# Dividing the last unit's attention sums through 16 turned columns, with the output operations behind the second sum and new tables of order

## The chip, the cores and the metric

The kernel runs on one core of a Trainium2 chip. A core has five engines that work side by side, each through its own list of instructions in order: TensorE (PE in the profile, its weight loads PEld), VectorE (DVE), ScalarE (ACT), GpSimd (POOL) and SyncE (SP), which here only issues DMA transfers. They wait for one another by semaphores. Matmul results land in PSUM, operands lie in SBUF, and large intermediates go through device memory. The metric is the device time of one execution in microseconds (us), lower being better.

## The reference

A token stream x of 2048 x 448 goes through two branches that a gate mixes:

```python
g = sigmoid((x * gate_w).sum(-1, keepdims=True))
a = ssm_conv(x)          # long convolution, kernel K from 448 x 256 complex exponentials
b = infini_attention(x)  # 16 heads of 28, 4 segments of 512 tokens, memory across segments
return g * a + (1 - g) * b
```

In branch b, for each segment s and head: p = softmax(q k^T * scale + causal mask); a_dot = p v; a_mem = phi(q) M / (phi(q) z + 1e-6); o = sigmoid(beta) * a_mem + (1 - sigmoid(beta)) * a_dot; then M and z take up phi(k)^T v and the sum of phi(k). The outputs of the heads are multiplied by wo.

## The kernel before

**First half (to about 440 us).** `first_half` builds the convolution kernel K in 56 steps: per step PE computes arguments (`turns`, ps_arg), ACT takes sines and exponentials (cs, EY, EX), DVE multiplies them into X and Y, and PE sums (`sums`, ps_k). Between these steps `Feed.slot` inserts pieces of another stream, `project`: it splits wv, wq and wk into a high and a low part (`weights`: a load win on SP, a copy wsp on ACT, a difference wsp on POOL, a store to WD on SP, with two wsp buffers), computes q, k and v, stores them (QD, KD, VD), and builds the memory. The tables say how much is inserted at each of 190 slots: FEED (pieces of `project`), FILL (pieces of the Fourier transform of x, "fill" matmuls ut,s1u), VECTOR (1: this slot's copies run on DVE, otherwise on ACT), and UNREAD (short matmuls into ps_k ahead of each `sums`, whose result nobody reads). CHUNKS places the transform of K.

**Second half.** The order is written out by hand in the string PROGRAM, one letter per piece: l loads the q and k of a unit (4 heads of one segment; 16 units), A and B are its maxima, W its scores and exponentials (five steps and one of masking on POOL), V its product with v, E a piece of a segment's end (division by sums, output projection into TB, recall of the memory), C the convolution, b, j and z the inverse transform, D the division of one unit of the last segment (`divide`). t and T are fillers on PE: t is a matmul on a tile of ones into a ps_m tile (`turn_over`), T two half-array ones into a ps_a tile (`turn_halves`). There are two ps_m and three ps_a tiles.

**The end.** `last_end` (L1312) finishes the last segment: it projects the units 0 to 2 of four output tiles, runs the last V (pvs, copied out of PSUM by ACT, L1194), divides unit 3, projects it, and adds the result to yd, which holds the convolution's part. In `divide` (L1298) one matmul with `den`, 128 x 512, spreads each head's sum of exponentials over its 32 rows; DVE takes the reciprocal of 256 columns (L1308), scales pvs (L1309) and adds the memory's part am (L1310), and the same for the other 256 columns.

The stream of instructions of an engine is in the order in which the code issues it wherever the code asks for that (all of PE, the two followed engines of the first half); elsewhere a scheduler places it.

## Time and profile before

| | us |
|---|---|
| runs shown (3) | 811.17, 814.91, 815.10 |
| median of the runs | 814.91 |
| profiled execution, its own time | 806.25 |
| its span, first to last instruction | 804.3 |
| mean granted clock of TensorE | 0.976 of full speed |

The profile is one execution. Its rows name the line, the engine, the operation and the tiles (out<-in, buffer numbers left out). L1503 and L1506 are the helpers that issue every matmul and transpose, L1468 and L1489 those for copies and activations, L1519 and L1527 those for DMA, so the tile names tell the place. A bracket behind a row gives the idle time of its engine ahead of it and what ended that. The granted clock is the share of full speed at which TensorE ran. An fp32 matmul appears as two passes, each with its weight load.

### The profile page before, as it was taken

What the parts mean: (1) busy time and instruction counts of PE and PEld (TensorE: products, weight loads), DVE (VectorE), ACT (ScalarE), POOL (GpSimd) and SP (SyncE); (2) the same over time, 40 slices, a digit from 0 to 9 for tenths busy, and PEclk for the clock granted to TensorE, in tenths of its full rate; (3) what the DMA queues carried; (4) which work ended last, traced back from release to release, by engine and by line L of the source; (5) the groups of instructions that cost most, each with busy time, mean ns of one, the idle gap of its engine ahead of it and who ended that gap; (6) DMA issues with size and microseconds to landing.
All of it is one profiled execution on the core that took longest, in us unless ns stands there. A gap on an engine that the chain in (4) does not pass through costs nothing.

```text
span 804.3 us, 18905 instructions
## 1 busy us (share of the span) xinstructions
PE 714.8 (89%) x7374; PEld 393.9 (49%) x7374; DVE 564.0 (70%) x1123; ACT 552.9 (69%) x649; POOL 263.5 (33%) x314
## 2 busy tenths in 40 slices
PE   1676798999877998799999999999899999999897
PEld 1353455666444754466656344444444445444343
DVE  6979498867877867699679745555455656576585
ACT  3878689999997899999986166665466736642230
POOL 5404311111021011201121145575556646563120
PEclk9988999999998999999999999999999999999799
DMA  8626884367573357652777948596667787675784
GB/s 213 173 65 203 256 274 130 104 175 228 159 227 115 127 150 225 210 169 75 208 241 266 335 148 255 182 325 209 224 238 244 230 265 231 212 255 230 199 278 154
DMA packets 111970, 165.05 MB, mean 205 GB/s; under 512 B 27234, under 2 KB 76442, under 8 KB 111834
## 3 DMA queue, kind: packets, MB, share of 16 engines
q1 hardware_dynamic: 100058, 150.29, 59.2%
q10 hardware_dynamic: 7936, 9.64, 3.6%
q0 software_dynamic: 3888, 3.93, 1.8%
q8 instruction: 58, 0.95, 0.5%
q14 instruction: 30, 0.25, 0.1%
HBM read 99.67 MB, written 60.63 MB: 199 GB/s over the span
## 4 chain that ended last, share of the span: by engine, by line
PE 56%; ACT 16%; DVE 12%; issue 7%; DMA 6%; POOL 2%; SPq 1%; ACTq 0%; DVEq 0%; POOLq 0%
PE ps_m L1503 24%; PE ps_a L1503 22%; ACT cs L1468 6%; PE ps_k L1503 5%; PE ps_arg L1503 4%; DVE Y L402 2%; ACT L1468 2%; PE ps_m L1506 2%; DVE jk L1125 2%; DVE X L398 2%; ACT EX L1468 2%; DVE Y L403 1%; DVE Y L404 1%; DMA WD<-wsp 1%; DVE pin_f L223 1%
## 5 line engine op out<-in xcount | busy, mean ns | idle before, releaser
L1125 DVE CUSTOM_DVE_ANT_0 jk<-ps_a,mk 128x512 f32<-128x512 f32 (+3 forms) x256 | 125.4, 490 | 45.3 <-PE ps_a L1503 35.2
L368 POOL TENSOR_TENSOR EX<-EX,cab 128x1024 f32<-128x1024 f32 x28 | 53.5, 1913 | 227.4 <-ACT EX L1468 207.7
L1164 ACT ACTIVATE PT<-ps_a 128x1024 f32<-128x1024 f32 x80 | 81.0, 1023 | 53.7 <-PE ps_a L1503 52.5
L1468 ACT ACTIVATE cs<-ps_arg 128x1024 f32<-128x1024 f32 x111 | 107.5, 1023 | 2.4 <-DVE Y L403 2.0
L1503 PE MATMUL ps_m<-xh,w 128*128 128x512 f32 x224 | 81.1, 416 | 3.4 <-DMA w<-WD 3.3
L398 DVE TENSOR_TENSOR X<-EX,cs 128x1024 f32<-128x1024 f32 x56 | 68.3, 1220 | 18.5 <-ACT cs L1468 17.4
L1173 POOL TENSOR_SCALAR_AFFINE_SELECT PT<-PT 128x256 f32<-128x256 f32 (+1 forms) x96 | 46.5, 495 | 85.9 <-ACT PT L1164 74.9
L711 POOL TENSOR_TENSOR pr<-us,ks 128x896 f32<-128x896 f32 x32 | 67.6, 2112 | 20.8 <-ACT us L710 20.6
L1503 PE MATMUL ps_k<-Y,X 128*32 128x64 f32 x3584 | 63.9, 224 | 8.9 <-DVE Y L403 8.1
L402 DVE TENSOR_TENSOR Y<-EY,cs 128x1024 f32<-128x1024 f32 x56 | 70.1, 1251 | 0.0
L1503 PEld LDWEIGHTS ps_k<-Y,X 128*32 128x32 f32 x3584 | 54.4, 112 | 26.7 <-DVE Y L403 12.2
L1503 PE MATMUL ps_a<-qu,ku 64*128 64x256 f32 (+3 forms) x512 | 62.0, 353 | 0.6 <-DVE mx L1125 0.4
L1468 ACT ACTIVATE cs<-cs 128x1024 f32<-128x1024 f32 x56 | 59.3, 1059 | 1.8
L1503 PE MATMUL ps_m<-wz 128*128 128x512 bf16 x171 | 53.0, 390 | 5.5 <-ACT tb L1267 3.5
L404 DVE SCALAR_TENSOR_TENSOR Y<-EY,cs 128x512 f32<-128x512 f32 x56 | 42.8, 765 | 19.5 <-ACT cs L1468 16.9
L1468 ACT ACTIVATE EY<-ps_arg 128x1024 f32<-128x1024 f32 x52 | 52.1, 1041 | 3.9 <-PE ps_arg L1503 3.7
L1503 PEld LDWEIGHTS ps_m<-xh,w 128*128 128x128 f32 x224 | 42.0, 187 | 25.7 <-issue 10.8
L1503 PEld LDWEIGHTS ps_a<-qu,ku 64*128 64x128 f32 x512 | 41.8, 186 | 25.8 <-issue 13.3
L1503 PE MATMUL ps_m<-xl,w 128*128 128x512 f32 x128 | 50.2, 392 | 0.0
L1503 PEld LDWEIGHTS <-lh 64*128 64x128 bf16 x392 | 19.1, 95 | 55.2 <-issue 43.8
L1503 PE MATMUL ps_arg<-ce,lh 64*128 64x512 bf16 x168 | 35.9, 407 | 9.2 <-ACT EY L1468 3.3
L1503 PE MATMUL ps_arg<-ct,lh 64*128 64x512 bf16 x224 | 37.3, 389 | 7.2 <-ACT cs L1468 4.7
(219 smaller groups left out, 1419.3 us busy)
## 6 DMA issues: line engine op xcount, KB each, us to landing
ku<-KD SPq DMA_DIRECT2D x30, 512.0 KB
w<-WD SPq DMA_DIRECT2D x32, 448.0 KB
qu<-QD SPq DMA_DIRECT2D x15, 512.0 KB
GU<-gs SPq DMA_DIRECT2D x32, 224.0 KB
gk<-GK SPq DMA_DIRECT2D x32, 224.0 KB
gu<-GU SPq DMA_DIRECT2D x32, 224.0 KB
BB<-bs ACTq DMA_DIRECT2D x16, 448.0 KB
bt<-BB SPq DMA_DIRECT2D x8, 896.0 KB
```

The source lines that it names most:

```text
L223: x = op(*args, **kw)
L368: nc.gpsimd.tensor_tensor(o, o, cab, ALU.mult)
L398: v.tensor_tensor(X, ex, t[:, :, 0], ALU.mult)
L402: v.tensor_tensor(Y[:, :, :, :32], lo, y[:, :, :, ::-1], ALU.mult)
L404: v.scalar_tensor_tensor(Y[:, 1, :, 32:], ey[:, :, 32:], -1.0, y[:, 1], ALU.mult, ALU.mult)
L711: nc.gpsimd.tensor_tensor(pr[c], us, ks.pop(c), ALU.mult)
L1125: v.tensor_tensor_reduce(junk[:, :n], pt[:, x, o : o + n], k.mk[:, SEG - n :], 1.0, -3e38, ALU.add, ALU.max, mx[:, 3 - t, h : h + 1],)
L1164: nc.scalar.activation(to, x, AF.Exp, scale=SCALE)
L1173: nc.gpsimd.affine_select(sl, sl, pat, ALU.is_ge, 0.0, base=0, channel_multiplier=-1)
L1468: x = op(*args, **kw)
L1503: tc.keep_in_program_order(nc.tensor.matmul(*args, **kw))
L1506: tc.keep_in_program_order(nc.tensor.transpose(*args))
```

## The change

1. `last_end` calls the new `divide_last` in place of `divide(3)`. It computes the sums turned: pvs is the stationary operand and 4 columns of `den` the moving one, so 128 tokens lie on the rows and the 16 sums of four token blocks in 16 columns. DVE takes one reciprocal of 128 x 16 and copies it out to 128 x 512 (each value 32 times); four matmuls with the identity turn that back into the layout of pvs, and DVE scales straight from PSUM. Half of a projection is issued between the copy and the turning.
2. The four operations that add to yd are issued behind the last sum (`issue_after(x.ins)`).
3. FEED, FILL, UNREAD, VECTOR and PROGRAM have new values. FILL's sum goes from 33 to 48, UNREAD's from 218 to 242, VECTOR's from 82 to 81; FEED's stays at 249. PROGRAM has 129 t and 90 T instead of 171 and 56. CHUNKS is the same.

```diff
 FEED = (
-    2, 1, 1, 1, 0, 0, 4, 0, 1, 5, 5, 1, 0,
+    1, 2, 1, 0, 0, 4, 1, 0, 1, 5, 6, 0, 0,
...
+    def divide_last(meanwhile):
+
+        hg = 3
+        o = pvss[3][:, hg]
+        ds = k.ps("m")
+        for t in range(4):
+            at = k.den.rearrange("p (j e) -> p j e", e=32)[:, :, 0]
+            k.mm(ds[:, 4 * t : 4 * t + 4], o[:, 128 * t : 128 * t + 128], at, start=True, stop=True)
+        rc = ap.tile([128, 16], F32, tag="rcd", name="rcd", bufs=2)
+        v.reciprocal(rc, ds[:, :16])
+        rs = ap.tile([128, SEG], F32, tag="jk", name="rcb", bufs=1)
+        v.tensor_copy(rs.rearrange("p (j e) -> p j e", e=32), rc.unsqueeze(2).broadcast_to([128, 16, 32]))
+        meanwhile()
+        pb = k.ps("m")
+        for t in range(4):
+            c = slice(128 * t, 128 * t + 128)
+            k.mm(pb[:, c], rs[:, c], k.ident, start=True, stop=True)
+        x = None
+        for h in range(2):
+            c = slice(256 * h, 256 * h + 256)
+            with k.issue_after(x.ins) if x else ExitStack():
+                v.scalar_tensor_tensor(o[:, c], o[:, c], k.omg[:, hg : hg + 1], pb[:, c], ALU.mult, ALU.mult)
+            x = v.tensor_tensor(o[:, c], o[:, c], am[3][:, hg, c], ALU.add)
+        return x
...
         project(0, [2])
-        divide(3)
-        project(1, range(2))
+        x = divide_last(lambda: project(1, range(1)))
+        project(1, range(1, 3))
         for h in range(2):
-            project(h, [2, 3] if h else [3])
+            project(h, [3])
             for t in (2 * h, 2 * h + 1):
                 po, yd, i = pos[t], yds[t], 12 + t
-                v.scalar_tensor_tensor(yd, po, k.ogt[:, i : i + 1], yd, ALU.mult, ALU.add)
+                with k.issue_after(x.ins):
+                    v.scalar_tensor_tensor(yd, po, k.ogt[:, i : i + 1], yd, ALU.mult, ALU.add)
...
-bAWEbttWEVtWEEAEEAttttWtAEWETbbtEtttVTTTEEjjjjj
+TbAWAEbttWEVWEEAWtETTEttATTTTAEtWETbTEbTTTVTTEEjjjjj
```

The last pair of PROGRAM lines is the stretch near 740 us, the end of segment 2: the 39th E of PROGRAM, which projects the first tile of that segment, is the fifth E of the line in both.

The last instructions of DVE before: rcb is the reciprocal, pvs the last unit, yd an output tile.

```order
L1308 RECIPROCAL rcb<-ps_m 128x256 [waits PE_49]
L1309 SCALAR_TENSOR_TENSOR pvs<-pvs,omg,rcb 128x256 [waits DVE_49,Activation_49]
L1310 TENSOR_TENSOR pvs<-pvs,am 128x256 [waits DVE_49]
L1308 RECIPROCAL rcb<-ps_m 128x256
L1309 SCALAR_TENSOR_TENSOR pvs<-pvs,omg,rcb 128x256 [waits DVE_49]
L1337 SCALAR_TENSOR_TENSOR yd<-ps_a,ogt,yd 128x448 [waits DMAHW5_49,PE_49]
L1337 SCALAR_TENSOR_TENSOR yd<-ps_a,ogt,yd 128x448 [waits DMAHW6_49]
L1310 TENSOR_TENSOR pvs<-pvs,am 128x256 [waits DVE_49]
L1337 SCALAR_TENSOR_TENSOR yd<-ps_a,ogt,yd 128x448 [waits DMAHW7_49,PE_49]
L1337 SCALAR_TENSOR_TENSOR yd<-ps_a,ogt,yd 128x448 [waits DMAHW0_49]
```

The last instructions of DVE after, with rcd the reciprocal of 16 columns:

```order
L1321 RECIPROCAL rcd<-ps_m 128x16 [waits PE_49]
L1323 COPY rcb<-rcd 128x512 [waits DVE_49]
L1333 SCALAR_TENSOR_TENSOR pvs<-pvs,omg,ps_m 128x256 [waits PE_49,Activation_49]
L1334 TENSOR_TENSOR pvs<-pvs,am 128x256 [waits DVE_49]
L1333 SCALAR_TENSOR_TENSOR pvs<-pvs,omg,ps_m 128x256
L1334 TENSOR_TENSOR pvs<-pvs,am 128x256 [waits DVE_49]
L1363 SCALAR_TENSOR_TENSOR yd<-ps_a,ogt,yd 128x448 [waits DMAHW5_49,PE_49]
L1363 SCALAR_TENSOR_TENSOR yd<-ps_a,ogt,yd 128x448 [waits DMAHW6_49]
L1363 SCALAR_TENSOR_TENSOR yd<-ps_a,ogt,yd 128x448 [waits DMAHW7_49,PE_49]
L1363 SCALAR_TENSOR_TENSOR yd<-ps_a,ogt,yd 128x448 [waits DMAHW0_49]
```

The first two output operations moved from ahead of the second sum to behind it.

On PE, the end before and after (PT,V is the last V, wo,pvs a projection of one unit and tile):

```order
L1503 MATMUL ps_m<-PT,V 32x128 x4
L1503 MATMUL ps_a<-wo,pvs 128x448 x2
L1503 MATMUL ps_m<-pvs,den 128x512
L1503 MATMUL ps_a<-wo,pvs 128x448 x10
L1737 UNCONDITIONAL_BRANCH
```

```order
L1529 MATMUL ps_m<-PT,V 32x128 x4
L1529 MATMUL ps_a<-wo,pvs 128x448 x2
L1529 MATMUL ps_m<-den,pvs 128x4 x4
L1529 MATMUL ps_a<-wo,pvs 128x448 x2
L1529 MATMUL ps_m<-ident,rcb 128x128 x4
L1529 MATMUL ps_a<-wo,pvs 128x448 x8
L1763 UNCONDITIONAL_BRANCH
```

Ten projections follow the sums in both; two of them now stand between the sums and the turning, eight behind it.

On SP near 70 us, before and after (WD is the store of split weights, win the load of wk, lh a small operand of `turns`):

```order
L1527 DMA WD<-wsp_220 64x4x128
L337 DMA lh_85<-SP 24x2x128
L1527 DMA WD<-wsp_220 64x4x128
L337 DMA lh_85<-SP 24x2x128 x3
L1527 DMA win<-in_B_wk 128x448 x3
L1527 DMA win<-in_B_wk 64x448 x2
L853 DMA w<-WD 128x896 x2
```

```order
L1553 DMA WD<-wsp_220 64x4x128
L1553 DMA win<-in_B_wk 128x448
L1553 DMA WD<-wsp_220 64x4x128
L1553 DMA win<-in_B_wk 128x448
L337 DMA lh_85<-SP 24x2x128 x4
L1553 DMA win<-in_B_wk 128x448
L1553 DMA win<-in_B_wk 64x448 x2
```

Two loads of wk moved ahead of the four lh loads.

On ACT at the same place, from the gs copy on, before and after:

```order
L1468 ACTIVATE gs<-ps_m 128x448
L1468 ACTIVATE cs<-ps_arg 128x2x2x256 x2
L1468 ACTIVATE cs<-cs 128x1024
L1468 ACTIVATE wsp_219<-win 128x4x4x28
L1468 ACTIVATE wsp_220<-win 128x4x4x28
L1468 ACT_TABLE_LOAD
L1468 ACTIVATE EY<-ps_arg 128x1024
```

```order
L1494 ACTIVATE gs<-ps_m 128x448
L1494 ACTIVATE wsp_219<-win 128x4x4x28
L1494 ACTIVATE wsp_220<-win 128x4x4x28
L1494 ACTIVATE cs<-ps_arg 128x2x2x256 x2
L1494 ACTIVATE cs<-cs 128x1024
L1494 ACT_TABLE_LOAD
L1494 ACTIVATE EY<-ps_arg 128x1024
```

The two wsp copies moved ahead of three cs activations.

## Prediction

> **What bounds the kernel now.** I read the page first, then a table of stretches, then the chain of waits at three places: the start, the pocket near 745 us, and the end.

> The head of the page, its share of the chain, and its row of granted TensorE clock in 40 slices (tenths of full speed):

> ```profile
> span 804.3 us, 18905 instructions
> PE 714.8 (89%) x7374; PEld 393.9 (49%) x7374; DVE 564.0 (70%) x1123; ACT 552.9 (69%) x649; POOL 263.5 (33%) x314
> ...
> PEclk9988999999998999999999999999999999999799
> ...
> PE 56%; ACT 16%; DVE 12%; issue 7%; DMA 6%; POOL 2%; SPq 1%; ACTq 0%; DVEq 0%; POOLq 0%
> ```

> TensorE (PE) is busy 89% of the span and carries 56% of the chain, so time is PE time, unless PE waits. The next table gives, for each stretch, its length and the busy time of PE, its weight loads, DVE, ACT and POOL, then the granted clock and the share of the DMA engines:

> ```profile
> 80.00:102.30 22.30, 16.66 (x129) 10.45 (x129) 10.96 (x14) 14.78 (x17) 7.27 (x5) 0.92 0.81 259
> 440.00:745.00 305.00, 296.79 (x1962) 140.50 (x1963) 179.55 (x594) 164.06 (x191) 165.13 (x213) 1.00 0.72 240
> 747.00:757.00 10.00, 10.00 (x53) 3.27 (x52) 3.19 (x5) 1.51 (x2) 2.45 (x5) 0.56 0.70 181
> 757.00:804.30 47.30, 41.70 (x241) 17.84 (x233) 33.18 (x44) 10.90 (x12) 5.82 (x11) 0.99 0.73 220
> ```

> The second half (from 440 us) has PE busy 296.8 of 305.0 us, but part of that is filler: the letters t and T of PROGRAM issue matmuls on a tile of ones whose result nobody reads. So a busy PE there is either at real work or covering a wait of another engine. Outside it three places matter: the start, where PE is idle 5.6 of 22.3 us; 747 to 757, where PE is busy throughout at a clock of 0.56; and the last 47 us, with 5.6 us of idle PE.

> **The change part by part.** The profiled execution took 806.25 us (span 804.3). The runs shown have a median of 814.91 us, 8.7 us above it, so I sum differences on the profiled execution and subtract them from the median.

> *Start: the wk split.* The chain there, in order of time (start, us, what):

> ```profile
> 72.43 5.20 DMA win<-in_B_wk
> ...
> 77.67 3.57 POOL wsp L837 x2
> ...
> 81.26 6.63 DMA WD<-wsp
> ...
> 87.99 0.58 ACT wsp L1468
> ```

> Four links follow one another: load of a block of wk, split on POOL, store to WD, and a copy of the next block which needs the freed buffer. The same in the timeline, with the wait that it puts on ACT in brackets, and the group row of an ACT copy to hi:

> ```profile
> 68.56 0.66 SPq L1527 DMA_DIRECT2D WD<-wsp  x1
> ...
> 73.42 0.54 ACT L1468 ACTIVATE gs<-ps_m 128x448 f32<-128x448 f32 x1 [2.63 <-PE ps_m L1503]
> ...
> 86.01 0.58 ACT L1468 ACTIVATE wsp<-win 128x448 fp32r<-128x448 f32 x1 [5.39 <-DMA WD<-wsp]
> ...
> 92.14 1.02 ACT L1468 ACTIVATE EX<-ps_arg 128x1024 f32<-128x1024 f32 x1 [0.83 <-PE ps_arg L1503]
> ```

> ```profile
> L1468 ACT ACTIVATE hi<-ps_m 128x512 fp32r<-128x512 f32 x13 | 7.8, 598 | 0.7 <-PE ps_m L1503 0.7
> ```

> ACT stands 5.39 us behind the store. In the changed FEED two of the wk loads leave SP directly behind the two small WD stores at 68.56 us, ahead of four small loads of lh; the load that the chain shows at 72.43 can then start at about 70.0, and the first two wsp copies stand behind gs (73.42) instead of behind three more cs activations. The chain gains about 72.43 - 70.0 = 2.4 us, and I add 0.1 for the first load, which lands earlier still: 2.5 us. Against it, ACT now waits for the load in front of cs work, and VECTOR moves two hi copies from DVE to ACT, 2 x 0.60 = 1.2 us, right behind the EX that follows the copy. One of the two fits into the 0.83 us that ACT waited at 92.14. Net -2.5 + 0.6 = **-1.9 us**. Bounds: -5.4, if the whole wait goes, and +1.2, if the earlier load only moves ACT's wait and both copies are paid. The lh loads that are passed are small and belong to later steps; I give them no price. Later moves in the first half (a fill matmul, a projection, a copy traded between ACT and DVE, 24 more short ps_k fillers in UNREAD) exchange equal work within a step or two; I put them at nothing, covered by ACT and PE which alternate as the bound; without cover a copy costs its 0.6 us.

> *Fillers of the second half.* A run of six t, a run of five T (two half-array matmuls each) and what follows:

> ```profile
> 455.19 1.47 PE L1503 MATMUL ps_m<-wz 128*128 128x512 bf16 x6
> 456.59 1.25 PE L1503 MATMUL ps_a<-wz 64*128 64x512 bf16 x10
> 457.50 0.59 PE L1503 MATMUL ps_a<-ku,qu 64*128 64x256 f32 x4
> ```

> From start to start a t costs (456.59 - 455.19) / 6 = 0.23 us and a T (457.50 - 456.59) / 5 = 0.18, so I take 0.23 for either. PROGRAM has 171 t and 56 T before, 129 and 90 after: 8 fewer. By place it is 5 more inside the pocket near 740 (below), 2 fewer at its end, and so 11 fewer elsewhere: at most 11 x 0.23 = 2.5 us. Where a filler covered a wait its loss buys nothing. No row says which; I take half, **-1.3 us**, between 0 and -2.5.

> *The pocket near 745.* Idle time and its cause stand in brackets; r<-RD is the DMA that POOL issues when the reciprocals of segment 3 have come back from memory:

> ```profile
> 733.73 0.79 PE L1503 MATMUL ps_a<-qu,ku 64*128 64x384 f32 x8
> 734.45 0.39 PE L1503 MATMUL ps_m<-wz 128*128 128x512 bf16 x1
> ...
> 738.00 0.53 POOL L1208 DMA_DIRECT2D r<-RD  x1 [4.91 <-DMA RD<-rs]
> ...
> 745.95 0.63 ACT L1267 ACTIVATE tb<-ps_m,ogt 128x448 f32<-128x448 f32 x1 [5.74 <-DMA TB<-tb]
> 746.63 0.59 PE L1503 MATMUL ps_m<-wz 128*128 128x512 bf16 x1 [3.53 <-ACT tb L1267]
> 747.15 0.79 PE L1503 MATMUL ps_m<-r,sel 8*128 8x512 f32 x1
> 747.87 1.46 PE L1503 MATMUL ps_m<-wz 128*128 128x512 bf16 x3
> ```

> POOL stands 4.91 us behind RD, so xt of the next tile is late, its store is late, ACT's tb waits 5.74 us for that store, and PE 3.53 us for tb. That chain starts at the output projection of tile 0 (39th E) and is untouched. The changed words put one step of scores (W, 734.45 - 733.73 = 0.72 us) ahead of it: the chain ends 0.72 us later. The t that stood at 746.63 is gone, 747.15 - 746.63 = 0.52 us, and one of six fillers behind it, 1.46 / 3 = 0.49 at this clock. Net 0.72 - 0.52 - 0.49 = **-0.3 us**. PE reaches the wait later by the 5 further fillers, 5 x 0.23 = 1.15 us, so it idles 3.53 + 0.72 - 1.15 = 3.1 us, which is still long.

> How long a wait lowers the clock shows at another place, an idle stretch and the one behind it:

> ```profile
> 338.80:341.40 2.60, 0.03 (x1) 0.00 (x0) 0.63 (x2) 2.53 (x4) 0.58 (x1) 1.00 0.63 224
> 342.50:345.00 2.50, 2.35 (x12) 1.99 (x12) 2.50 (x4) 2.47 (x4) 0.00 (x0) 0.56 0.50 170
> ```

> After 2.6 us of idle PE the granted clock was 0.56, so I leave the 0.56 of 747 to 757 as it is. [...]

> *The end.* The chain, then three durations for the new operations: a reciprocal of 16 columns, a one-pass SBUF operation of 512 columns, and eight passes of 128 columns with what follows them on PE:

> ```profile
> 789.90 0.87 PE ps_m L1503 x2
> ...
> 790.80 1.77 DVE rcb L1308
> ...
> 793.61 1.68 DVE rcb L1308
> ...
> 796.98 0.34 DVE pvs L1310
> ...
> 797.37 2.54 PE ps_a L1503 x6
> ```

> ```profile
> 790.60 5.58 PE L1503 MATMUL ps_a<-wo,pvs 128*128 128x448 f32 x14
> ```

> ```profile
> L1050 DVE RECIPROCAL gt<-gt 128x16 f32<-128x16 f32 x1 | 0.3, 253 | 0.0
> ```

> ```profile
> L896 DVE TENSOR_SCALAR e<-e 128x512 f32<-128x512 f32 x24 | 10.3, 464 | 4.6 <-ACT e L1468 4.6
> ```

> ```profile
> 150.13 1.16 PE L1503 MATMUL ps_m<-v,pkT 128*128 128x128 f32 x8 [0.32 <-ACT pkT L1468]
> 151.04 0.46 PE L1503 MATMUL ps_m<-wvh,xh 128*128 128x450 f32 x1
> ```

> Before: sums of exp ready at 790.77, two reciprocals of 1.77 and 1.68 us on DVE, and PE idle until the second half is added (797.32); six passes then end at 799.91. After: four matmuls of 4 columns (8 passes) replace the one of 512. Eight passes of 128 columns take 151.04 - 150.13 = 0.91 us, and PE can hardly go slower with 4 columns, so the sums stand at about 790.8 as before. The reciprocal is 0.25 us, the copy 0.46 (to 0.7): rs is there at 791.7. PE meanwhile does four passes of projection; 14 passes in 5.58 us are 0.40 at most, so it is free at 792.3. The turning takes another 0.91, to 793.2, and two scale and add pairs of 0.95 us end at 794.2 and 795.1. PE still has 16 passes, 6.4 us, hence to 799.6, and never meets the later sums: the bound at the end passes from DVE to PE. 799.91 - 799.6 = 0.3; since 0.40 a pass is an upper bound (0.37 would make it 0.9), I take **-0.5 us**. The output operations now stand behind the second sum, where two of them stood ahead of it. The price is that the first two stores leave about 2 us later, close to the last two: up to +0.5 if the four share the way out. Bounds of this part: -1.2 and +0.8 (PE at twice 0.91 for the new matmuls).

> Sum: -1.9 - 1.3 - 0.3 - 0.5 = **-4.0 us**, that is 806.25 to 802.2, and 814.9 to **810.9 us**.

> **The rivals.** *A: only the end counts.* The tables exchange work that some other wait hides, at the start because SP's loads, with the DMA engines at 0.81 of their time (80 to 102 us), arrive no earlier. Then -0.5: 814.4 us. For it: the amounts of work on every engine are the same. Against it: the 5.39 us on ACT have one named cause, and that is moved.

> *B: the pocket gets short enough for the clock.* If 3.1 us of idling keeps the clock, the 10 us at 0.56 give back 10 x 0.44 = 4.4 us: 810.9 - 4.4 = 806.5 us. [...] Against it stands the row with 2.6 us.

> *C: slower, by the ps_a buffers.* T takes one of three ps_a tiles, which scores and maxima also take, where t takes ps_m. The runs of T go from 33 to 43 and those of t from 94 to 79. If every new run of T waits for one reader of its buffer (an exp on ACT takes 1.02 us by the EX row's size), that is 10 x 1.02 = 10.2, and -4.0 + 10.2 = +6.2: 821.1 us. It decides from 4.0 / 10 = 0.4 us a run on. Against it: PE's row of the second half shows 8 us idle in 305, with 33 such runs in it.

> **How the numbers follow.** 0.5% of 814.9 is 4.1 us, about what a measurement of this kernel can tell from no change. My forecast has 0.45: its own range is -7.5 to -1.5 (start between -4.4 and -0.5, fillers between 0 and -2.5), 807.4 to 813.4, and the sum lies at the edge, so it splits into 0.23 faster and 0.22 same. A has 0.18 (same), B 0.15 (faster), C 0.17 (slower); 0.05 is for what I name in none of them, 0.03 of it faster and 0.02 slower. Together faster 0.41, same 0.40, slower 0.19. The range reaches past B by some of the forecast's own width and halfway to C: 803 to 818.

> **What would show each step.** Start: ACT's wait of wsp for WD under 3.5 us and the first PE work behind the third w load about 2 us ahead of 102.3. Fillers: PE idle from 440 to 745 us grows by less than 1.3 us while the stretch gets shorter. Pocket: PE's wait for tb near 3 us and a clock near 0.56 behind it (B: near 1.00). End: no PE idle between the sums and the last projection, and the output operations directly behind PE. The prediction is wrong if T's own waits in ps_a add up to over 4 us (C), if ACT's wait at the start only moves to the wk load, or if a new idle of PE of over 2.6 us appears with a half clock behind it.

## The result and the profile after

| | before | changed |
|---|---|---|
| median of 17 runs each, side by side | 814.55 us | 805.70 us |
| lowest and highest | 808.66, 817.97 | 800.71, 810.18 |
| the profiled execution, its own time (span) | 806.25 (804.3) | 810.18 (808.5) |

The ratio is 0.990 (95% interval 0.9876 to 0.9923): 8.9 us faster by the medians, 8.1 us by the ratio. A second set, 12 runs of the changed kernel against 23 of the one before, gave 0.9927 (0.9898 to 0.9955). So the gain lies at 6 to 9 us (the two intervals reach from 3.7 to 10.1), and the prediction (-4.0 us, range 803 to 818) had the sign and was about half the size. Of all executions shown here one, of the kernel with the covered pocket below, took 1321.34 us and is left out of its ratio and its median.

The two profiled executions say the opposite: the changed kernel's span is 4.2 us longer. They are one execution each, and from opposite ends: 806.25 lies below all 17 runs of before, and 810.18 is the slowest of the 17 of the changed kernel. Subtracting these spans would have led astray, so in what follows a stage is compared over all the executions that a profile was taken of (14 in the end).

The head of the page of the changed kernel, and its four stretches (length, busy us of PE, weight loads, DVE, ACT and POOL, granted clock, DMA share and GB/s):

```profile
span 808.5 us, 19012 instructions
...
PEclk9987999999999999999999999999899999999889
...
PE 50%; ACT 20%; DVE 12%; DMA 7%; issue 6%; SPq 2%; POOL 2%; ACTq 0%; DVEq 0%; POOLq 0%
```

```profile
80.00:102.30 22.30, 18.18 (x137) 10.63 (x136) 10.32 (x14) 16.96 (x20) 6.09 (x4) 0.95 0.88 281
440.00:745.00 305.00, 291.94 (x1959) 141.79 (x1974) 179.15 (x588) 163.26 (x190) 164.85 (x212) 0.99 0.71 236
745.00:757.00 12.00, 11.19 (x61) 3.96 (x59) 4.18 (x7) 3.29 (x5) 2.44 (x5) 0.59 0.71 181
757.00:808.50 51.50, 43.68 (x240) 19.73 (x240) 30.36 (x44) 9.75 (x11) 5.82 (x11) 0.93 0.67 200
```

The start has 1.5 us more PE work in the same 22.3 us. The clock behind the pocket is about as low as before (0.59). New is the last row: a clock of 0.93 in the last 51 us, where before had 0.99.

**Where the time went, stage by stage.** The marks are starts of rows: the 5th, 13th, 21st and 29th multiplication X on DVE (L398), the first maximum jk (L1125, the second half begins), the 97th, 161st and the last jk, the first matmul of the last V, and the end of the span. The means are taken over profiled executions of all kernels below: in the first five rows over those whose first half is wholly old or wholly new, in the next four over those with the old or the new PROGRAM (without the three that edit the pocket or a load of bt), in the last over those with the old or the new end:

| stage | old | new | difference, us |
|---|---|---|---|
| start to 5th X | 98.07 (3) | 96.22 (7) | -1.9 |
| 5th to 13th X | 53.12 | 56.76 | +3.6 |
| 13th to 21st X | 53.98 | 54.62 | +0.6 |
| 21st to 29th X | 58.13 | 53.42 | -4.7 |
| 29th X to first jk | 178.98 | 177.54 | -1.4 |
| first to 97th jk | 90.10 (6) | 87.99 (5) | -2.1 |
| 97th to 161st jk | 88.89 | 89.98 | +1.1 |
| 161st to last jk | 127.41 | 127.53 | +0.1 |
| last jk to last V | 41.82 | 43.03 | +1.2 |
| last V to the end | 18.48 (7) | 17.82 (7) | -0.7 |

In brackets is the number of executions; it holds for the rows below it up to the next bracket. The first half gains 3.8 us, most of it between the 21st and the 29th X, in a place to which the prediction gave nothing. The words (PROGRAM) gain 2.1 us at the beginning of the second half, and the later rows have it back. The end gains what it was predicted to.

### The profile page after: what moved, and what is told of

It is laid out like the page before. It is cut to its first block, busy times and chain, and to the rows that moved or that the text cites. A ratio compares the mean times of both kernels' runs of the same rounds, so it can differ in the third digit from the quotient of the medians.

```text
span 808.5 us, 19012 instructions
## 1 busy us (share of the span) xinstructions
PE 713.1 (88%) x7415; PEld 398.9 (49%) x7438; DVE 561.3 (69%) x1122; ACT 552.5 (68%) x650; POOL 263.5 (33%) x314
## 4 chain that ended last, share of the span: by engine, by line
PE 50%; ACT 20%; DVE 12%; DMA 7%; issue 6%; SPq 2%; POOL 2%; ACTq 0%; DVEq 0%; POOLq 0%
PE ps_m L1529 21%; PE ps_a L1529 21%; ACT cs L1494 7%; PE ps_k L1529 4%; DVE jk L1125 4%; PE ps_arg L1529 3%; ACT L1494 2%; DVE X L398 2%; PE ps_m L1532 2%; DVE Y L402 2%; ACT EX L1494 2%; SPq L337 1%; ACT EY L1494 1%; DMA bt<-BB 1%; DVE Y L403 1%
## 5 line engine op out<-in xcount | busy, mean ns | idle before, releaser
L1125 DVE CUSTOM_DVE_ANT_0 jk<-ps_a,mk 128x512 f32<-128x512 f32 (+3 forms) x256 | 125.4, 490 | 50.8 <-PE ps_a L1529 41.1
L398 DVE TENSOR_TENSOR X<-EX,cs 128x1024 f32<-128x1024 f32 x56 | 69.3, 1237 | 18.4 <-ACT cs L1494 17.5
L404 DVE SCALAR_TENSOR_TENSOR Y<-EY,cs 128x512 f32<-128x512 f32 x56 | 40.7, 727 | 18.3 <-ACT cs L1494 15.9
L1529 PE MATMUL ps_a<-ku,qu 64*128 64x512 f32 (+3 forms) x256 | 41.7, 383 | 1.8 <-DVE mx L1125 1.3
L1140 POOL DMA_DIRECT2D qu<-mn x64 | 32.6, 516 | 29.4 <-ACT mn L1135 27.0
```

Of the source, the lines that this page charges most:

```text
L398: v.tensor_tensor(X, ex, t[:, :, 0], ALU.mult)
L404: v.scalar_tensor_tensor(Y[:, 1, :, 32:], ey[:, :, 32:], -1.0, y[:, 1], ALU.mult, ALU.mult)
L1125: v.tensor_tensor_reduce(junk[:, :n], pt[:, x, o : o + n], k.mk[:, SEG - n :], 1.0, -3e38, ALU.add, ALU.max, mx[:, 3 - t, h : h + 1],)
L1140: k.pdma(q[r : r + 1].bitcast(F32), mn[2 * j : 2 * j + 2, b].bitcast(F32))
L1529: tc.keep_in_program_order(nc.tensor.matmul(*args, **kw))
```

## The experiments

Each was timed beside the kernel before on the same chip. Ratios are to before. They are taken from all the runs of a set and are not the quotient of the medians; the medians of before were 812.71 us in the set of the first table below, 812.77 in that of the second table and of the covered pocket, and 813.49 in the last. The kernels have 12 runs each, where nothing else is said.

**Which part carries it.** Four kernels take the change apart: the new division and output order with all old tables; all new tables with the old division; the first half's tables alone (FEED, FILL, UNREAD, VECTOR); PROGRAM alone. The edit of the first as a diff against the kernel before is the diff of the functions shown above without the tables; of the second:

```diff
-        x = divide_last(lambda: project(1, range(1)))
-        project(1, range(1, 3))
+        divide(3)
+        project(1, range(2))
         for h in range(2):
-            project(h, [3])
+            project(h, [2, 3] if h else [3])
```

> Only the last unit's division and the place of the output operations are changed; all five tables are those of before. The two profiles at hand give, from the start of the last V's product on PE to the end of the span, 804.3 - 785.9 = 18.4 us before and 808.5 - 790.7 = 17.8 us after. Theory 1 (the terms of the prediction were each too small): about -0.6 us, no difference that can be measured, 811 to 816 us at a median of before of 814.5. Theory 2 (the end carries the gain): -4 us or more. Theory 3 (the gain is the tables'): 0, like theory 1.

> All five new tables, with the old division of the last unit. Theories 1 and 3: -8 us against before, so the new tables alone make it faster, about 806.5 us. Theory 2 (the end carries half or more): -4 us or less, 810 us or later.

> Only FEED, FILL, UNREAD and VECTOR are new: the first half; the words and the end are those of before. The prediction's start term is -1.9 us and it gives the other moves of the first half nothing, so by it 812.6 us. Theory 3a (the first half carries the gain, because the start's whole wait of 5.39 us goes and the later moves gain too): -5 us or more, 809.5 us or less. Theory 3b (the words carry it): -2 us or less.

> Only PROGRAM is new: the order of the second half. The prediction's terms for it are -1.3 us (fillers) and -0.3 us (pocket), so 812.9 us. Theory 3a: as that, -1.6 us or less. Theory 3b (the words carry the gain, by fewer waits or by a clock that keeps longer): -5 us or more, 809.5 us or less. If the parts are independent, end_alone, first_alone and words_alone add up to about -8.9 us.

| kernel | median | ratio to before |
|---|---|---|
| the end alone | 812.77 | 0.9982 (0.9955 to 1.0009) |
| the end undone | 806.76 | 0.9935 (0.9909 to 0.9962) |
| the first half's tables alone | 808.34 | 0.9953 (0.9924 to 0.9983) |
| PROGRAM alone | 813.01 | 0.9994 (0.9972 to 1.0016) |

The end does not carry the gain (theory 2 falls). The first half does (0.0047 x 813 = 3.8 us, theory 3a, though less than the 5 us it named), and PROGRAM by itself is worth nothing that can be measured: 0.5 us, in an interval from 2.3 faster to 1.3 slower, which also holds the 1.6 us of the prediction. Its profile does have the last V 2.7 us closer to the first jk (343.2 against 345.9 us); the lower half of the stage table shows what becomes of that.

**Which part of the first half.** FEED's running sums of before and after meet at many slots, so the tables can be exchanged in pieces. Three kernels on the base of before: slots 0 to 21 with the first ten numbers of UNREAD (the start); slots 73 to 85 (the middle, which acts between the 21st and the 29th X); slots 86 to 189 with UNREAD from the 15th number on (the rest of the first half). The new numbers of slots 22 to 72, among them one more transform of x at slot 31, and the 14th of UNREAD are in none of the three. The middle, in full, over slots 73 to 85 of each table:

```diff
-FEED    0, 1, 3, 2, 1, 1, 1, 1, 1, 0, 1, 1, 0
+FEED    0, 1, 0, 1, 3, 3, 0, 2, 1, 0, 1, 1, 0
-FILL    0, 0, 0, 0, 0, 1, 0, 0, 0, 0, 0, 0, 0
+FILL    1, 0, 0, 0, 0, 1, 0, 0, 0, 0, 0, 0, 1
-VECTOR  0, 1, 1, 1, 0, 0, 0, 1, 1, 1, 1, 0, 0
+VECTOR  1, 0, 1, 1, 0, 0, 0, 1, 1, 1, 1, 0, 0
```

> Before, with the new numbers of the first 22 slots of FEED and VECTOR and the first 10 of UNREAD, up to where FEED's sums meet again (21 pieces): the wk loads and copies of the start. In three profiles of the old first half the step of X that holds the start's wait (from the 4th to the 5th X on DVE) took 20.7, 21.9 and 19.4 us, in three of the new one 18.1, 17.4 and 17.9. Theory S (the prediction's start term, a little larger): that step takes about 18 us, and the time falls by 2 to 3 us, about 810.5 us. Theory M (the later moves of the first half carry it): the step gets shorter, but the next steps give it back, and the time falls by less than 1.5 us.

> Before, with the new numbers of FEED, FILL and VECTOR in slots 73 to 85 only: one transform of x more at slot 73 and one at 85, and eight pieces of the projection some slots later. Before, PE idled 3.25 us at 245 us behind DVE, with a half clock behind it, and the steps of X from the 26th to the 29th took 25.4 us (26.3 and 26.6 in two more profiles); in the changed kernel 22.2. Theory M: these three steps fall to about 22 to 23 us, the half clock there goes, and the time falls by 3 to 4 us, about 809.5 us. Theory S: no more than 1 us.

> Before, with the new numbers of FEED, FILL and VECTOR from slot 86 on and of UNREAD from the 15th on. In the profiles the steps from the 29th X to the first maxima of the second half took 179.4, 179.2 and 178.4 us with the old tables and 177.1, 177.5 and 177.5 with the new ones. Both theories: -1.5 to -2 us, which the profile shows and five rounds hardly do (812.5 us); -4 us or more would mean that the late moves carry the gain.

| kernel | median | ratio to before |
|---|---|---|
| the start alone | 809.26 | 0.9980 (0.9950 to 1.0009) |
| the middle alone | 809.03 | 0.9955 (0.9929 to 0.9982) |
| slots 86 on alone (6 runs) | 824.06 | 1.0130 (1.0102 to 1.0159) |

The middle, two transforms of x, seven pieces of the projection moved by one or two slots (by a count of FEED) and two numbers of VECTOR, gives 0.0045 x 812.8 = 3.7 us by itself, as theory M said. What it does is seen on PE. First before, then the kernel with the middle alone (start, us, engine, line, operation, tiles; idle time and its cause in brackets):

```profile
243.71 1.10 PE L1503 MATMUL ps_k<-Y,X 128*32 128x64 f32 x64
244.75 0.39 PE L1503 MATMUL ps_arg<-ce,lh 64*128 64x512 bf16 x2
248.39 1.11 PE L1503 MATMUL ps_m<-ut,s1u 64*128 64x448 f32 x1 [3.25 <-DVE lo L882]
248.40 1.03 PE L1503 MATMUL ps_arg<-ce,lh 64*128 64x512 bf16 x2
```

```profile
246.88 1.10 PE L1503 MATMUL ps_k<-Y,X 128*32 128x64 f32 x64
247.91 0.60 PE L1503 MATMUL ps_arg<-ce,lh 64*128 64x512 bf16 x3
248.14 0.91 PE L1503 MATMUL ps_m<-ut,s1u 64*128 64x448 f32 x2
248.89 0.92 PE L1503 MATMUL ps_arg<-ce,lh 64*128 64x512 bf16 x3
```

Before, the transform (ut,s1u) needs a ps_m tile which DVE frees only with lo, and all of PE stands in order behind it. DVE's copy of the transform ahead of it, gs, which frees another such tile, comes later still; in the kernel with the middle alone it comes 2.9 us earlier, so that its tile is free in time (before, then the middle alone):

```profile
248.25 0.61 DVE L1468 COPY gs<-ps_m 128x448 f32<-128x448 f32 x1
```

```profile
245.31 0.61 DVE L1468 COPY gs<-ps_m 128x448 f32<-128x448 f32 x1
```

ACT's next operation is the copy of the waiting transform's result, so ACT stands too (before):

```profile
250.28 0.54 ACT L1468 ACTIVATE gs<-ps_m 128x448 f32<-128x448 f32 x1 [4.08 <-PE ps_m L1503]
```

With the middle changed the transform finds its tile free, and neither waits. The stall was followed by 6.8 us at a granted clock of 0.50 (247.2 to 254.0 us), and that is gone as well, as a stretch that ends ahead of the same v,pkT shows in both (before, then the middle alone; the stretch does not begin with the same work):

```profile
235.00:261.00 26.00, 19.86 (x325) 11.54 (x313) 21.10 (x32) 20.65 (x25) 3.82 (x2) 0.87 0.34 111
```

```profile
235.00:259.50 24.50, 19.86 (x351) 12.24 (x351) 23.80 (x35) 23.82 (x29) 3.83 (x2) 1.00 0.52 160
```

From the transform ahead of the stall to that v,pkT it is 261.5 - 239.3 = 22.2 us before and 259.9 - 242.4 = 17.5 with the middle alone. The other profiles agree: between the 21st and the 29th X all five kernels with the old middle have a wait of PE for lo of 2.7 to 3.5 us (3.0 us and at an earlier transform where the start alone is new), and in none of the nine with the new middle does PE wait more than 1.8 us there. Which of the three tables' numbers does it was not separated.

The rest of the first half alone was the surprise: 11 us slower, where either theory had 2 us faster. Its profile loses 8 us between the 37th and the 45th X against the changed kernel and 5.4 against before (58.8, 50.8 and 53.4 us), where six passes, three transforms of x, stand from 351.27 on that the changed kernel has done before this place; DVE, with their copies, frees ps_m tiles late, and PE waits:

```profile
351.27 1.40 PE L1503 MATMUL ps_m<-ut,s1u 64*128 64x448 f32 x3
...
367.46 0.66 PE L1506 MATMUL ps_m<-ident,xin 128*128 128x128 f32 x4 [1.36 <-DVE lo L882]
370.84 1.11 PE L1506 MATMUL ps_m<-ident,xin 128*128 128x128 f32 x4 [2.73 <-DVE lo L884]
```

In the changed kernel the first of these waits is not there and the second is 0.24 us. Two of these three transforms are the middle's, and the third is that of slot 31. With all three moved ahead the changed kernel has issued all 32 transforms by 336 us (40th X), so that the new numbers of FILL from slot 144 on (43rd X) find nothing left; in the kernel with slots 86 on alone they draw the last three together. So the new numbers from slot 86 on seem to rest on the earlier ones; the pieces do not add up, and pieces of such a table cannot be priced one by one. That the missing three transforms are the whole reason was not tried, and 3.5 us of the loss lie elsewhere, between the 21st and the 29th X (61.6 us, where the mean of the old is 58.1).

**The start, in the whole.** The changed kernel with the old numbers in slots 0 to 21, beside a repeat of the changed kernel:

> The changed kernel with the old numbers in the first 22 slots of FEED and VECTOR and the first 10 of UNREAD: it undoes the start alone. Theory S (the start's earlier wk loads are worth 2 to 3 us in the whole): 2 to 3 us slower than the changed kernel, about 808 us, and the step from the 4th to the 5th X back at 19.4 to 21.9 us. Theory M (what the start gains the next steps give back): within 1 us of the changed kernel.

> The changed kernel itself, for a second profile and for a comparison on the same chip with the three kernels beside it. All theories: about 0.990 of before, 804 to 807 us; -0.5% or less would mean that its first measurement was lucky.

Undone: 809.98 us, 0.9968 (0.9947 to 0.9989); the changed kernel: 806.62 us, 0.9927 (0.9898 to 0.9955). The start is worth 0.0041 x 813 = 3.3 us in the whole, with intervals that just overlap, and -1.6 us (-4.1 to +0.7) by itself; by the times theory S, 2 to 3 us, fits both. The profiles support it in the whole alone: the step from the 4th to the 5th X is 22.2 us with the start undone and 16.9 to 19.9 in the seven kernels with all of the new first half, but 20.1 with the start alone, where theory S had 18, and the 5th X stands there at 99.0 us, within the 97.3 to 99.6 of the six with the old start. So what the start gains by itself is not shown.

**The pocket: does the clock matter?** In the changed kernel the idle time of the pocket stands between two T and ahead of the recall r,sel:

```profile
741.13 0.49 PE L1529 MATMUL ps_m<-r,sel 8*128 8x512 f32 x1
741.56 0.39 PE L1529 MATMUL ps_a<-wz 64*128 64x512 bf16 x2
744.46 0.60 PE L1529 MATMUL ps_a<-wz 64*128 64x512 bf16 x2 [2.51 <-DVE mx L1125]
745.88 0.79 PE L1529 MATMUL ps_m<-r,sel 8*128 8x512 f32 x1 [0.81 <-ACT tb L1267]
```

The second T starts a new run, so it takes a new ps_a tile and waits for DVE's reading of the old one. One long run needs no second tile and can cover the whole wait:

```diff
-...ATTTTAEtWETbTEbTTTVTTEEjjjjj
+...ATTTTAEtWETTTTTTTTTTTTTTTTTTTTbEbTTTVTTEEjjjjj
```

> The changed kernel with one further edit: in the pocket near 745 us the two T, which stand in two runs around a load and so take two ps_a tiles, become one run of 20 T in one tile, which waits for no second buffer and covers PE's idle time there (2.51 + 0.81 us in the profile of the changed kernel) with 40 half-array matmuls of 0.12 us, 4.7 us in all. Theory H (a window of 3.41 us in which PE idles for more than about half is followed by a half clock; the 10.2 us at half clock behind this pocket come from there): the clock behind the pocket stays full and the time falls by up to 5 us against the changed kernel's 805.7, about 801 to 803 us. Theory N (the stretch behind the pocket does not hang on PE, or the clock falls anyway): 805 to 807 us.

Measured 809.00 us (11 runs), 0.9961 (0.9936 to 0.9986): no faster than the changed kernel with its 0.990 and 0.993, if anything slower. Yet the edit did to the clock what theory H said. The 3.4 us with the idle time and the 10 us behind them, in the changed kernel and then with the cover:

```profile
741.10:744.50 3.40, 0.89 (x6) 0.33 (x5) 3.33 (x8) 0.00 (x0) 1.55 (x3) 1.00 0.14 54
744.50:754.70 10.20, 9.39 (x39) 3.06 (x42) 4.68 (x7) 2.14 (x3) 1.99 (x5) 0.50 0.61 165
```

```profile
739.50:742.90 3.40, 3.40 (x30) 1.56 (x31) 3.33 (x8) 0.00 (x0) 1.15 (x2) 1.00 0.20 72
742.90:753.00 10.10, 9.95 (x81) 4.09 (x77) 5.09 (x8) 3.74 (x5) 2.85 (x6) 1.00 0.64 170
```

What PE gained it lost at the next thing that it waits for, the last of eight loads bt<-BB (z's input, bt,fc on PE). PE with the cover, and SP, which issues that load:

```profile
772.95 1.72 PE L1529 MATMUL ps_a<-bt,fc 128*64 128x448 f32 x8
779.12 3.18 PE L1529 MATMUL ps_a<-bt,fc 128*64 128x448 f32 x8 [4.44 <-DMA bt<-BB]
```

```profile
758.97 0.55 SPq L1545 DMA_DIRECT2D bt<-BB  x1
765.41 1.12 SPq L1545 DMA_DIRECT2D rest<-TB  x2
...
770.69 0.56 SPq L1545 DMA_DIRECT2D bt<-BB  x1
```

There are five bt buffers, so the last load needs that of the third z, which PE had read at 758.9 us. It leaves SP at 770.7: ahead of it in SP's order stands a load of rest, which SP issues at 765.4 after nothing since 759.5, and then eight issues of stores. The changed kernel's profile has the same wait, of 2.94 us, with a clock of 0.50 behind it (782.06 to 788.89 us); this is the 0.93 of its last row above. To tell whether this load hides the pocket, it was put on POOL's queue, without and with the cover:

```diff
-        k.dma(bts[wc], bv[:, :, 2 * wc : 2 * wc + 2])
+        (k.pdma if wc == 7 else k.dma)(bts[wc], bv[:, :, 2 * wc : 2 * wc + 2])
```

> The changed kernel with the last of the eight loads bt<-BB issued on POOL's queue, where it stands ahead of the masks of the last unit, and not on SP's, where it stood behind a load of rest that waits for a buffer (SP issued nothing from 759.5 to 765.4 us in the run with the covered pocket). PE waited 2.94 us for this load in the profile of the changed kernel, and 4.44 us with the covered pocket, but not in the profile of before. Theory H (the load sets the pace of the end as soon as PE gets there early): the wait goes, 1 to 4 us faster than the changed kernel, about 803 us. Theory N: no difference, 805 to 807 us.

> Both edits: one run of 20 T in the pocket, and the last load of bt on POOL's queue. Theory H (the full clock behind the pocket is worth 3 to 5 us, and was hidden by the wait of 4.44 us for that load): no half clock behind the pocket, no wait for bt, and 4 to 7 us faster than the changed kernel, 799 to 802 us. Theory N (the stretch behind the pocket does not hang on PE): 804 to 807 us.

| | load on SP | load on POOL |
|---|---|---|
| pocket as changed | 0.9927 (0.9898 to 0.9955), 806.62 us | 0.9901 (0.9871 to 0.9932), 805.75 us |
| pocket covered | 0.9961 (0.9936 to 0.9986) | **0.9848 (0.9824 to 0.9873), 800.55 us** |

The covered pocket with the load on SP was timed in another set than the other three; the load on POOL has 6 runs, both edits together have 4. Neither edit alone is measurably faster than the changed kernel (the load alone takes the wait for bt away, but its time is that of theory N); both together make 800.55 us, 6.1 us faster than the changed kernel beside it and 12.9 us faster than before. That is theory H. PE then runs through:

```profile
760.85 0.77 POOL L756 DMA_DIRECT2D bt<-BB  x1 [0.42 <-PE ps_a L1529]
```

```profile
741.56 4.49 PE L1529 MATMUL ps_a<-wz 64*128 64x512 bf16 x40
746.05 0.49 PE L1529 MATMUL ps_m<-r,sel 8*128 8x512 f32 x1
...
774.61 3.23 PE L1529 MATMUL ps_a<-bt,fc 128*64 128x448 f32 x16
777.76 3.27 PE L1529 MATMUL ps_a<-wo,pvs 128*128 128x448 f32 x8
```

Counted from the start of the T run, the load leaves after 19.3 us (760.85 - 741.56) where it left after 30.7 with the cover alone (770.69 - 739.96), the last two z run in one piece, and from the pocket to the last projection PE has no wait over 0.6 us. Eight passes of bt,fc take 1.72 us at all six places ahead of this piece, where the last eight took 3.18 us behind the wait with the cover alone.

## Why the prediction was right in sign and short in size

**The size of the whole.** The 805.70 us of the first set lie outside the forecast's own range (807.4 to 813.4) and inside the stated one only because that was drawn past rival B, which did not come by itself; that the stated range holds the result is luck. (The ends of the own range add up to -7.7 and -1.3, where -7.5 and -1.5 are stated.)

**The start (-1.9) came out in size; its two signs did not.** The stage to the 5th X is 1.9 us shorter in the mean, and the runs give 1.6 to 3.3 us, but the start alone does not show it in its profile (above). ACT's wait was to fall under 3.5 us, and the first PE work behind the third w load to come 2 us ahead of 102.3. In the changed profile they are 4.70 us and 0.8 us ahead:

```profile
84.86 0.58 ACT L1494 ACTIVATE wsp<-win 128x448 fp32r<-128x448 f32 x1 [4.70 <-issue]
```

```profile
101.47 0.47 PE L1529 MATMUL ps_m<-xh,w 128*128 128x512 f32 x1 [0.59 <-DMA w<-WD]
```

The chain there, with the load and the store that follow each other:

```profile
71.00 3.23 DMA win<-in_B_wk
...
78.63 7.58 DMA WD<-wsp
```

The load starts at 71.0, 1.4 us ahead of before's 72.43 (the forecast had 70.0), and lands at 74.2 us, before's at 77.6. The store leaves 2.6 us earlier and then took 7.58 us where before it took 6.63: part of the lead went into the transfer.

**The step that failed: "Later moves in the first half ... exchange equal work within a step or two; I put them at nothing, covered by ACT and PE which alternate as the bound".** They do exchange equal work, but between the 21st and the 29th X that exchange took away a stall of 3.25 us with its half clock (-4.7 us in the mean, 3.7 us in the runs), and between the 5th and the 21st it cost 4.2 us. Most of that cost lies between the 5th and the 13th X, with the new numbers of slots 22 to 72: the six kernels with the old ones take 52.1 to 54.1 us there and the eight with the new ones 55.3 to 58.9, and PE's wait near 141 us for ACT's gs copy is 1.7 to 2.1 us in the six and 2.8 in the eight. No kernel changes these slots alone, so which of their numbers does it stays open. In the trace of before the stall was PE's longest between 70 and 440 us, and the change put two transforms ahead of it. What was missing is the question that was put to the pocket: which tile does the waiting matmul need, who frees it, and does the change move either of them?

**The fillers (-1.3) bought nothing that the runs can show.** The first 96 jk are 2.1 us shorter in every execution (87.95 to 88.04 us against 90.08 to 90.13), close to the bound of -2.5. The later stages have it back in the means, though part of that is chance: the marker "PE idle grows by less than 1.3 us" came out wrong (305.0 - 291.9 = 13.1 us against 8.2; 2.5 of it is the pocket's wait, which before lies behind 745 us), and one stall near 575 us, PE behind DVE's mn, was followed by a clock of 0.50 in the changed kernel and 0.51 in its repeat (1.89 and 1.65 us of idle PE in the 3.4 us ahead), and of 1.00 in before and in the kernel with the covered pocket (1.51 and 1.45 us); from the 97th to the 161st jk the changed kernel took 90.7 us and before 87.4.

**The pocket (-0.3) and rival B.** The idle time was put at 3.1 us and measured 2.51 + 0.81 = 3.3, and the clock behind it fell as forecast (0.50 for 10.2 us). But only 0.81 us of it is the wait for tb; in the other 2.51 a T waits for its ps_a tile, which is rival C's mechanism, ahead of the wait that was forecast. Rival B priced a kept clock at 4.4 us, with nothing said of who is late next. The cover kept the clock (1.00) and gave nothing; with the load of bt out of the way it gave 805.75 - 800.55 = 5.2. Rival B was about right in the price and blind to the load. The prediction also named a new idle time of PE of over 2.6 us with a half clock behind it as a sign that it is wrong; in the changed kernel's profile this sign came true, as the 2.94 us for bt.

**Rival C came in part.** T's own waits between 440 and 745 us sum to 3.3 us in 170 half-array matmuls, most of it the one in the pocket, where C needed 10. All waits of PE for a ps_a tile behind DVE's mx grow there from 2.2 to 6.1 us, still well under C's price. The T in the changed kernel:

```profile
L1529 PE MATMUL ps_a<-wz 64*128 64x512 bf16 x170 | 25.7, 382 | 3.3 <-DVE mx L1125 3.2
```

**Rival A** (only the end counts) fell with the tables: without the new end the kernel still has 0.9935.

**The end (-0.5) measured -0.66** in 7 profiles against 7 (18.48 to 17.82 us, each within 0.1), and -1.5 us (-3.6 to +0.7) by the runs. The chain is the one that was forecast:

```profile
790.74 2.29 PE ps_m L1529 x32
793.03 1.70 PE ps_a L1529 x4
794.73 0.79 PE ps_m L1529 x8
795.52 1.61 PE ps_a L1529 x4
797.13 0.89 PE ps_m L1529 x8
798.02 6.03 PE ps_a L1529 x16
804.05 0.03 issue
804.08 0.68 DVE yd L1363
```

From the last V on it is PE without a gap: the turned sums (8 passes of 4 columns) take 0.79 us where 0.91 was assumed, the turning back 0.89 (0.91), and 16 passes 6.03 (6.4).

Added up: -1.9 at the start, about -2 for the rest of the first half with both its signs (-3.8 in all), nothing that shows for the words where -1.6 stood, -0.7 for the end. That makes -4.5 us by the stages, -5.8 by the ratios of the three parts (0.18 + 0.47 + 0.06 = 0.71% of 814), and -6 to -9 by the whole. The rest is within what these intervals leave open; no run here assigns it to a place.

## What to carry to other kernels

In a table-driven order, look for the longest stalls of the tensor engine first and ask of each whether the change moves the waiting instruction, or the one that frees its tile; equal work exchanged elsewhere says nothing about them. A stall that is covered, or a clock that is kept, is worth what the next wait leaves of it: name that wait, and test the two edits together, since either alone can measure as nothing. When executions scatter by 1%, compare stages over several profiles and never the spans of two.

## What the runs showed of the hardware

```profile
138.00:141.40 3.40, 2.10 (x14) 1.27 (x15) 3.40 (x7) 3.40 (x6) 0.00 (x0) 1.00 0.95 268
141.40:144.80 3.40, 3.40 (x82) 2.28 (x82) 3.40 (x7) 2.69 (x4) 1.92 (x1) 1.00 0.62 225
```

```profile
138.50:141.90 3.40, 1.41 (x10) 0.62 (x8) 3.40 (x7) 3.40 (x6) 0.00 (x0) 1.00 0.71 190
141.90:145.30 3.40, 3.40 (x16) 2.52 (x14) 3.13 (x6) 2.16 (x3) 1.91 (x1) 0.50 0.88 331
```

Idle 1.30 us, and the clock stays at 1.00; idle 1.99 us, and it is 0.50. In before the wait, 2.00 us up to 139.30, lies across an edge at 137.98. Much of the scatter of these runs, 800.7 to 810.2 us for one kernel, may come from such half clocks; the time and the mean clock of the changed kernel's 17 runs go against each other with a correlation of -0.63.
